# Attention and maxout feed-forward on one core: bias products as units of their own, first loads in quarters, twelve result buffers, and a new queue

## The chip, the cores and the metric

The kernel runs on one core of a Trainium2 chip. Its time is the device time of one execution in microseconds (us), lower is better. A profile is one execution taken by the hardware profiler; engines are called TensorE (PE, with PEld for its weight loads), VectorE (DVE), ScalarE (ACT), GpSimd (POOL) and SyncE (SP, which here issues nearly all DMAs).

## What is computed

A windowed attention with global keys (4 batches, 8 heads, 768 positions, head size 64), then a feed-forward layer with a maximum over three products. Cut to its core:

```python
scores = scale * q @ k.T                       # 4 x 8 heads, 768 x 768, head size 64
keep   = (pos_k < 8) | ((0 <= rel) & (rel < 96))
bias   = -slopes[h] * where(is_global & ~is_local, 96, abs(rel))
a      = softmax(where(keep, scores + bias, -1e9))
x      = (a @ v) as 3072 x 512
h      = maximum(maximum(x @ w1, x @ w2), x @ w3)    # 3072 x 768
out    = h @ w_out                                    # 3072 x 512, float32
```

## The kernel before, in words

Positions are worked on in 24 tiles T of 128 (six for each batch). A tile needs scores against itself and the tile before it; tile 0 of a batch only against itself. The eight global keys and values of a batch are copied over rows of the preceding tile's keys and values that are out of the window anyway. Tiles are gathered into chunks of 4, 2, 2, 4, 4, 4, 4 for the feed-forward part; `c` below is the chunk, `f` one of six blocks of 128 hidden columns, `j` one of the three weight matrices.

The order of all work is written out by hand (by a planner outside this file) in one string, `SCHEDULE`. Each word is a unit: a letter, its arguments, and after `@` the slot of the ring (buffer) that it writes. Each engine gets its instructions in the order of that string and runs them strictly in that order; semaphores between engines follow from the buffers. The units that matter here:

- `l a.G.p`: load a (0 q, 1 k, 2 v) of the pair of tiles G. The first two pairs of q and k come as one group of four tiles, `QUAD` = 12, split by heads into parts p: 0 and 1 are halves (512 KB), 2 and 3 quarters. `c a.G.p.how` casts it to bf16; `v T.e.how` casts values; `how` is the engine: 0 ScalarE, 1 VectorE, 2 GpSimd.
- `x G.a.p` and `y G.a.p.how`: transposes on TensorE and the copy out of PSUM into `qkT`. Later pairs use `X T`, a transposing DMA.
- `G T.how`, `V T.e.how`: the copies of global keys and values. `G T` has to stand behind the scores of tile T, `V T` behind its products with v.
- `S T.g.how`: scores of four heads (g is 0 or 1). Where `how` is 1, two matmuls with the identity first put the bias into PSUM, and the mask product is not needed.
- `e T.g`: exponential on ScalarE. `m T.g`: product with the mask `wmask`. `A T`: product with v. `n T`: normalization. `t`/`u` or `Z`: transpose of x.
- `K h`, `B h.how`: rows of `wmask` and of `bias`. `D n.w`: n dummy matmuls of width w.
- `w g.j`, `W g.j.how`: load and cast of weights (g = 0: 256 columns, 512 KB, blocks f 0 and 1; g = 1: 512 columns, 1 MB, cast in two units W1 and W2 for blocks 2, 3 and 4, 5). `q`, `Q`: the same for w_out.
- `F c.f.j` (four matmuls, "gate product") and `f c.f.j.how`: the products of the three matrices and the maximum. `O c.tt` (six matmuls), `o` and `s`: the product with w_out of one tile, the copy out of PSUM, the store. `E`: the products, copies and stores of the last chunk in one unit, the last tile in pieces of 256, 128 and 128 columns; the last piece's store goes out from ScalarE's queue.

Result tiles lie in the staging rings of the weights, `wst0` and `wst1`, of three slots each.

Of the kernel before, what the change touches and what calls it, by code (L numbers as in the profile page):

```python
# [29 lines left out]
    v2.1.1 v2.0.1 A0@0 n0@0 v3.0.2 l2.2.2@2 w1.1@1 A1@4 V1.1.2 e2.0@5 v3.1.2 n1@1 S3.0.1@6 c0.2.2.0@2 V1.0.1  # L30
    S3.1.1@0 w1.2@2 t1@2 c1.2.2.1 u1.1@0 e3.0@6 A2@4 n2@2 x2.0.2@3 V2.1.2 V2.0.2 x2.1.2@2 G3.2 y2.1.2.1@2
    e3.1@7 l1.3.2@6 A3@0 t2@4 l0.3.2@0 y2.0.2.0 W0.1.2 n3@3 t0@3 u2.0 S4.0.0@6 u0.1 e4.0@1 S4.1.0@4 t3@2
    u3.1 W0.0.1 G4.2 S5.0.0@0 W0.2.2 e5.0@3 S5.1.0@6 m5.0.1 V3.1.0 e5.1@0 m5.1.1 m4.0.1 W2.0.1 v5.0.2 e4.1@2
    W1.0.1 F0.0.1@2 F0.1.1@3 F0.0.0@0 f0.0.0.0@0 F0.1.0@1 F0.0.2@4 F0.1.2@0 f0.1.0.0@1 F0.4.0@1 v5.1.2
    V3.0.1 F0.3.0@5 m4.1.1 f0.0.1.1 f0.1.1.1 f0.1.2.1@0 v4.0.0 v4.1.0 F0.2.0@2 f0.3.0.0@2 A4@6 F0.5.0@0
    V4.0.0 l2.3.2@0 W2.1.1 W1.1.2 q1@0 W1.2.0 F0.4.1@3 l1.4.2@1 f0.0.2.1 n4@1 F0.5.1@4 c1.3.2.2@1 V4.1.1
    f0.2.0.0@3 A5@6 f0.4.0.1@4 F0.3.1@1 l0.4.2@2 t4@5 n5@2 F0.2.1@6 t5@2 F0.3.2@7 f0.5.0.0@1 F0.2.2@0 u4.1@1
    f0.2.1.1 f0.3.1.1 f0.5.1.1 u5.0 c0.3.2.0 F1.0.1@1 F1.4.0@2 x3.0.2@6 F1.2.0@4 W2.2.0 f0.2.2.1 f0.4.1.1
    f1.4.0.0@0 q2@1 f0.3.2.1 v6.1.2 v7.0.2 q0@2 y3.0.2.0@3 F1.0.0@0 f1.0.0.0@3 f1.0.1.1 F1.4.1@5 v6.0.2
    l2.4.2@1 x3.1.2@7 Q1.2 l1.5.2@3 F0.5.2@0 c1.4.2.2@0 F1.0.2@1 v7.1.2 f1.4.1.1 y3.1.2.0 G6.0 c0.4.2.2  # L40
    f1.2.0.0@2 f0.5.2.1 f1.0.2.1@1 F1.2.1@5 f1.2.1.1 Q0.2 S6.0.0@2 e6.0@4 l0.5.2@4 S7.0.0@6 S7.1.0@0
    S6.1.0@4 F0.4.2@2 f0.4.2.1 e7.1@5 F1.5.0@3 F1.1.0@0 m7.1.1 e7.0@6 m7.0.1 F1.3.0@1 F1.5.1@2 x4.1.2@6
    f1.5.0.0@1 F1.2.2@3 m6.0.1 f1.2.2.1 v8.1.2 l1.6.2@5 e6.1@7 m6.1.1 x4.0.2@7 f1.5.1.1 f1.1.0.0@3 F1.1.1@0
    f1.1.1.1 f1.3.0.0@4 y4.1.2.0@0 A7@4 V7.0.2 v9.0.2 G7.0 v9.1.2 F1.3.1@1 n7@0 y4.0.2.0 Q2.0 c1.5.2.0@2
    F1.4.2@0 f1.4.2.1 f1.3.1.1 F1.5.2@2 S8.1.0@4 S8.0.0@6 f1.5.2.1 G8.0 A6@0 O0.2@2 n6@3 O0.3@3 e8.1@1 Z7@2
    o0.3.1@0 e8.0@2 o0.2.0@0 t6@0 c0.5.2.2 v8.0.2 u6.1 m8.1.1 V7.1.1 m8.0.1 O0.1@1 o0.1.1@1 S9.1.0@2 e9.1@0
    m9.1.1 S9.0.0@4 G9.1 e9.0@3 F2.0.0@0 F2.5.0@6 F1.1.2@7 F1.3.2@1 F2.3.0@2 f1.1.2.1 m9.0.1 l2.5.2@2 A8@4
    v11.1.0 V8.0.0 V8.1.2 F2.2.0@3 f2.3.0.0@2 f2.2.0.0@0 f2.5.0.1@1 f1.3.2.1 n8@1 l0.6.2@6 F2.3.1@7 f2.3.1.1
    F2.2.1@1 f2.2.1.1 F2.4.0@6 c0.6.2.0@1 f2.0.0.0@3 A9@2 n9@2 v10.1.1 c1.6.2.2 X10@1 S10.0.0@4 e10.0@5
    V9.1.1 m10.0.1 S10.1.0@0 e10.1@6 V9.0.0 G10.1 O1.1@7 F2.5.1@2 f2.5.1.1 t8@3 F2.4.1@0 O0.0@1 m10.1.1 X11  # L50
    S11.1.0@4 l1.7.2@0 f2.4.0.0@4 o1.1.0@2 e11.1@4 v11.0.0 u8.1@0 S11.0.0@2 v10.0.1 f2.4.1.1 A10@6 V10.0.2
# [37 lines left out]
RINGS = {'r': 7, 'rv': 3, 'qb': 3, 'qkT': 4, 'sp': 2, 'h': 8, 'P': 8, 'xb': 4, 'xT': 3, 'wst0': 3, 'wst1': 3, 'ht': 2, 'h01': 5, 'rz': 4}  # L89

LAST_BANKS = (7, 6, 4, 5, 2, 0, 3, 1)

LAST_STAGES = ((2, 1, 0), (2, 0, 1))


@with_exitstack
def kernel(
# [13 lines left out]
    nc = tc.nc  # L111
# [24 lines left out]
    for name in RINGS:  # L136
        if name not in ("h", "sp"):
            pools[name] = ctx.enter_context(tc.tile_pool(name=f"p_{name}", bufs=1))
# [42 lines left out]
    def cast(how, dst, src):  # L181

        n = src.shape[1]
        for lo, hi in (((0, n // 2), (n // 2, n)) if how == 2 else ((0, n),)):
            copies[how](dst[:, lo:hi], src[:, lo:hi])  # L185
# [400 lines left out]
```

## Time and profile before

| what | value |
|---|---|
| time, median of 3 runs (lowest, highest) | 176.48 us (176.45, 177.07) |
| the profiled execution's own time | 176.6 us |
| its span, first to last instruction | 174.7 us |
| busy, share of the span: PE, DVE, ACT, POOL | 96%, 73%, 59%, 28% |
| granted TensorE clock, mean | 1.000 |
| instructions | 3862 |

Times in the profile count from the span's start. A row of a group reads: line, engine, operation, tiles, count, then busy us in all and mean ns of one, then the engine's idle time just before them with what ended it.

### The profile page before, as it was taken

The page shows a single profiled execution, that of the slowest core. Times are in us where ns is not written, and L with a number is a line of the kernel's source. Part 1 is how long each engine was busy: PE and PEld are TensorE (multiplying, and loading weights), DVE is VectorE, ACT ScalarE, POOL GpSimd, SP SyncE. Part 2 cuts the span into 40 slices and gives each one's busy share as a digit, 9 for nine tenths or more (in the row PEclk, how much of TensorE's full clock was granted, in tenths as well). Part 3 has the DMA queues.
Part 4 walks back from the last instruction along what each step waited for, and adds up shares of the span by engine and source line. Part 5 has one row for each costly group of instructions (what it writes and reads, how often), then busy time and mean ns, then how long its engine had stood idle before and what let it go on. Part 6 is the DMA issues. An engine that isn't in the chain of part 4 may idle for free.

```text
span 174.7 us, 3862 instructions
## 1 busy us (share of the span) xinstructions
PE 166.9 (96%) x1489; PEld 93.5 (54%) x1510; DVE 127.7 (73%) x259; ACT 102.4 (59%) x153; POOL 48.9 (28%) x94
## 2 busy tenths in 40 slices
PE   7799999999999999999999999999999999999992
PEld 2346745576956867644456445554444554444442
DVE  7798969784868988589697287839859993059930
ACT  5979895487995876746257994721375651310022
POOL 4056536349370300196614003200203210000000
PEclk9999999999999999999999999999999999999999
DMA  5999999999999898998989498999992134047106
GB/s 148 352 292 312 363 351 379 294 319 345 270 230 267 193 145 194 290 319 198 232 146 196 119 253 200 290 159 260 272 184 68 32 90 64 0 180 240 60 10 234
DMA packets 66658, 37.35 MB, mean 214 GB/s; under 512 B 24144, under 2 KB 61904, under 8 KB 66640
## 3 DMA queue, kind: packets, MB, share of 16 engines
q1 hardware_dynamic: 66496, 37.04, 84.5%
q8 instruction: 12, 0.20, 0.5%
q10 hardware_dynamic: 144, 0.07, 0.1%
q14 instruction: 6, 0.05, 0.1%
HBM read 25.17 MB, written 6.29 MB: 180 GB/s over the span
## 4 chain that ended last, share of the span: by engine, by line
PE 83%; DVE 5%; DMA 4%; ACT 3%; issue 2%; SPq 1%; ACTq 0%
PE psum L405 50%; PE psum L429 18%; PE psum L321 5%; DMA rawqq<-in_q_dram 4%; PE psum L363 4%; PE psum L366 3%; PE psum L258 2%; DVE qkT L266 1%; ACT P L328 1%; PE psum L390 1%; DVE h L421 1%; DVE P L337 1%; PE psum L313 1%; SPq L213 1%; ACT qb L185 1%
## 5 line engine op out<-in xcount | busy, mean ns | idle before, releaser
L405 PE MATMUL psum<-xT,w 128*128 128x512 bf16 (+1 forms) x491 | 99.3, 348 | 1.1
L405 PEld LDWEIGHTS <-w 128*128 128x128 bf16 x504 | 47.5, 98 | 43.1 <-issue 2.7
L328 ACT ACTIVATE P<-psum 128x1024 bf16<-128x1024 f32 (+1 forms) x48 | 43.3, 953 | 13.5 <-PE psum L321 13.2
L421 DVE TENSOR_TENSOR h<-h,psum 128x512 bf16<-128x512 bf16 (+1 forms) x42 | 24.6, 604 | 16.1 <-PE psum L405 12.6
L429 PE MATMUL psum<-wo,ht 128*128 128x512 bf16 (+2 forms) x148 | 32.9, 362 | 0.6 <-issue 0.3
L337 DVE TENSOR_TENSOR P<-P,wmask 128x1024 bf16<-128x1024 bf16 x35 | 23.8, 695 | 6.2 <-ACT P L328 6.1
L424 DVE TENSOR_TENSOR ht<-h,psum 128x512 bf16<-128x512 bf16 (+1 forms) x42 | 26.1, 643 | 3.0 <-PE psum L405 2.4
L419 ACT CAST h<-psum 128x512 bf16<-128x512 f32 (+1 forms) x32 | 15.6, 517 | 20.1 <-PE psum L405 17.9
L429 PEld LDWEIGHTS <-ht 128*128 128x128 bf16 x156 | 14.0, 98 | 14.1
L238 POOL CAST va<-rawv 64x512 bf16<-64x512 f32 x26 | 16.5, 636 | 13.6 <-DMA rawv<-in_v_dram 12.8
L375 DVE TENSOR_TENSOR xb<-psum,rz 128x512 bf16<-128x512 f32 x24 | 16.6, 691 | 0.8
L299 POOL COPY va<-vaf 4x260 int32<-4x260 int32 x15 | 5.9, 395 | 37.5 <-PE psum L366 37.2
L321 PE MATMUL psum<-qkT 64*128 64x128 bf16 x352 | 14.9, 217 | 1.2 <-DVE qkT L266 0.9
L321 PEld LDWEIGHTS <-qkT 64*128 64x128 bf16 x352 | 10.3, 94 | 9.6 <-issue 6.8
L363 PEld LDWEIGHTS <-P 128*128 128x128 bf16 x192 | 12.3, 97 | 2.4
L363 PE MATMUL psum<-va,P 128*128 128x65 bf16 x160 | 12.5, 193 | 0.1
L444 ACT COPY ost<-psum 128x512 f32<-128x512 f32 x11 | 6.4, 589 | 8.9 <-PE psum L429 8.2
L366 PEld LDWEIGHTS <-P 128*128 128x128 bf16 x160 | 10.4, 97 | 1.5 <-issue 0.3
L434 ACT COPY ost<-psum 128x512 f32<-128x512 f32 (+2 forms) x5 | 2.3, 480 | 15.1 <-PE psum L429 15.0
L366 PE MATMUL psum<-va,P 128*128 128x65 bf16 x128 | 9.9, 193 | 0.0
L301 ACT COPY va<-vaf 4x520 bf16<-4x520 bf16 x10 | 6.2, 620 | 3.8 <-PE psum L366 3.7
L374 DVE RECIPROCAL rz<-psum 128x8 f32<-128x8 f32 x24 | 4.8, 202 | 4.7 <-PE psum L366 3.7
(69 smaller groups left out, 134.4 us busy)
## 6 DMA issues: line engine op xcount, KB each, us to landing
rawv<-in_v_dram SPq DMA_DIRECT2D x12, 512.0 KB, 6.3
rawq<-in_q_dram SPq DMA_DIRECT2D x10, 512.0 KB, 7.3
rawk<-in_k_dram SPq DMA_DIRECT2D x10, 512.0 KB, 7.0
out_dram<-ost SPq DMA_DIRECT2D x19, 256.0 KB, 2.6
wst<-in_moe_w_dram SPq DMA_DIRECT2D x3, 1024.0 KB, 10.9
wst<-in_moe_w_dram SPq DMA_DIRECT2D x3, 512.0 KB, 8.1
wost<-in_moe_w_out_dram SPq DMA_DIRECT2D x3, 512.0 KB, 7.3
out_dram<-ost SPq DMA_DIRECT2D x9, 128.0 KB, 1.8
```

The lines of the kernel that those rows point to most:

```text
L238: copies[how](heads(va(T))[64 * e:64 * e + 64, :, 0:D], src)
L321: nc.tensor.matmul(sp[:, hh, j2, ds], qT(T - ds, 1)[hsl, jp], qT(T, 0)[hsl, jp], start=not how, stop=True, skip_group_check=True)
L328: nc.scalar.activation(P[:, :, 0:n], sps[T, g].rearrange("p a b d n -> p (a b) d n")[:, :, 0:n], AF.Exp, bias=0.0, scale=scale)
L337: mul(P, P, wmask[:, g, :, 0:2])
L363: nc.tensor.matmul(o, P[:, i, 0], heads(va(T))[:, h], start=True, stop=(t == 0), skip_group_check=True)
L366: nc.tensor.matmul(o, P[:, i, 1], heads(va(T - 1))[:, h], start=False, stop=True, skip_group_check=True)
L375: nc.vector.tensor_tensor(out=x.rearrange("p (g h) d -> p g h d", g=2), in0=o4[:, :, :, 0:64], in1=rz[:, :, :, None].to_broadcast([128, 2, ...
L405: nc.tensor.matmul(ps, w123[f // 2][:, j, dm, (f % 2) * 128:(f % 2) * 128 + 128], xT[c][:, dm], start=(dm == 0), stop=(dm == 3))
L419: copies[how](h01, ps)
L421: nc.vector.tensor_max(h01s[c, f], h01s[c, f], ps)
L424: nc.vector.tensor_max(dst, h01s[c, f].rearrange("p (t e i) -> p t e i", e=2, i=64), ps.rearrange("p (t e i) -> p t e i", e=2, i=64))
L429: nc.tensor.matmul(po, ht[c][:, f, tt * 128:(tt + 1) * 128], wo[:, f, cols], start=(f == 0), stop=(f == NF - 1))
```

## The change

- A new unit `b T.g` holds the two bias matmuls of a score unit; it takes the PSUM slot, and `S T.g.1` then adds the scores onto it. The seven biased units are 0.0, 0.1, 1.0, 2.0, 2.1, 3.0, 3.1, as before.
- The second loads of q and k of `QUAD` (part 0) are replaced by two quarters each (parts 2 and 3), with their casts and transposes; `cast` can split a quarter for GpSimd.
- Results are copied to a ring `os` of twelve buffers of 512 columns, which lies over the memory of `wst1`; `wst0` and `wst1` become parts of one tile `staging`.
- `SCHEDULE`, `LAST_BANKS` and `LAST_STAGES` are new. Dummy matmuls: before `D10.512 D3.256 D3.256`, then `D10.512 D1.256 D3.256 D3.256 D3.256 D2.256`. In the middle casts and copies change engines (fewer on GpSimd), and at the end one whole result tile of chunk 5 (`O5.0 o5.0.0 s5.0.2`) stands behind `E`.

```diff
 SCHEDULE = """
-    l0.12.1@0 l1.12.1@1 R K4 K3 K6 B4.1 B0.1 K5 K0 K2 B1.0 K7 B6.0 B2.1 l1.12.0@2 B3.1 c0.12.1.1@0 B7.1
-    l0.12.0@3 l2.0.2@0 l2.1.2@1 l0.2.2@4 c1.12.1.1@1 l1.2.2@5 w0.1@0 B5.1 D10.512@0 w0.0@1 x12.0.1@0
-    y0.0.1.0@0 w0.2@2 D3.256@1 x12.1.1@1 y0.1.1.1 S0.1.1@2 c1.12.0.1 c0.12.0.1 S1.1.0@4 K1 x12.1.0@6
-    y0.1.0.1 G0.2 y1.0.1.0@1 e1.1@0 m1.1.1 v0.0.2 v1.0.2 e0.1@1 v0.1.2 D3.256@0 x12.0.0@0 y0.0.0.0 S1.0.1@2
-    w1.0@0 G1.0 e1.0@2 y1.1.0.1 S0.0.1@4 e0.0@3 y1.1.1.1 y1.0.0.1 S2.1.1@6 e2.1@4 v1.1.2 S2.0.1@2 G2.2
...
+    l0.12.1@0 l1.12.1@1 R K7 D10.512@0 l1.12.2@2 l0.12.3@3 l1.12.3@4 l0.12.2@5 K3 K0 K5 K1 K2 K6 K4 B6.1
+    B1.0 B7.2 B5.1 c0.12.1.1@0 D1.256@0 x12.0.1@0 B2.1 B4.1 c1.12.1.1@1 B0.0 c1.12.2.2 l2.0.2@0 b0.1@2
+    x12.1.1@1 y0.0.1.1@0 l2.1.2@1 b2.1@4 y0.1.1.0 D3.256@6 S1.1.0@6 c0.12.3.1 y1.0.1.0@1 S0.1.1 c1.12.3.2
+    v0.1.2 y1.1.1.1 v1.1.2 v0.0.2 v1.0.2 e1.1@0 l1.2.2@6 c0.12.2.1 B3.1 x12.1.2@0 x12.0.3@1 x12.1.3 x12.0.2
+    y0.1.0.0 l0.2.2@0 b1.0@6 y0.0.0.1 S1.0.1 G0.1 G1.1 e0.1@1 y1.0.0.1 b0.0@2 S2.1.1 m1.1.1 y1.1.0.0 S0.0.1
+    b2.0@0 S2.0.1 v3.1.2 e1.0@2 e0.0@3 e2.1@4 v2.1.1 G2.1 w0.0@0 v2.0.1 b3.0@2 w0.1@1 e2.0@5 D3.256@6 A1@4
+    V1.0.1 A0@6 v3.0.2 c1.2.2.2@2 V1.1.1 w1.0@0 n1@0 S3.0.1 b3.1@0 S3.1.1 e3.0@6 e3.1@7 t1@4 G3.0 n0@1
+    l2.2.2@2 A2@2 V2.0.2 w0.2@2 V2.1.2 t0@5 u0.0@0 c0.2.2.1 w1.1@1 x2.1.2@6 n2@2 x2.0.2@7 y2.1.2.0@2
+    y2.0.2.1 A3@0 w1.2@2 u1.0 n3@3 D3.256@2 S4.1.0@2 e4.1@0 l1.3.2@1 S4.0.0@4 G4.1 t2@6 u2.0 W0.0.1 t3@7
...
-    f6.0.1.1 f6.0.2.1 f6.3.2.1 s4.0.2 s4.3.2 s5.2.2 F6.5.0@0 f6.5.0.1@0 F6.5.1@3 f6.5.1.1 F6.5.2@1 f6.5.2.1 E@0
+    f6.1.1.1 f6.1.2.1 F6.2.2@0 F6.5.0@2 f6.2.2.1 f6.5.0.1@1 F6.5.1@1 f6.5.1.1 f6.5.2.1 o5.2.1@9 s5.2 s4.3.2
+    E@3 O5.0@1 o5.0.0@6 s5.0.2
 """
-RINGS = {... 'wst0': 3, 'wst1': 3, ...}
+RINGS = {... 'wst0': 3, 'wst1': 3, ..., 'os': 12}
-LAST_BANKS = (7, 6, 4, 5, 2, 0, 3, 1)
-LAST_STAGES = ((2, 1, 0), (2, 0, 1))
+LAST_BANKS = (5, 4, 3, 0, 2, 7, 6, 1)
+LAST_STAGES = (11, 0, 4, 1, 10, 3, 2, 7, 8, 9, 5, 6)
...
+    staging = persist.tile([128, 2048 * RINGS["wst1"] + 1024 * RINGS["wst0"]], FP32, name="staging")
+    staged = {"wst1": (0, 2048), "os": (0, 512), "wst0": (2048 * RINGS["wst1"], 1024)}
...
-    def u_S(slot, T, g, how):
-        t = T % NT
+    def u_b(slot, T, g):
+
+        n = 2 if T % NT else 1
         sp = ring("sp", slot, [128, 2, 2, 2, 128], FP32, "sp")
         sps[T, g] = sp
-        n = 2 if t else 1
+        for hh in range(2):
+            nc.tensor.matmul(sp[:, hh, :, 0:n], identb, bias[:, g, hh, :, 0:2] if n == 2 else bias[:, g, hh, :, 2:3],
+                             start=True, stop=False, skip_group_check=True)
+
+    def u_S(slot, T, g, how):
+        n = 2 if T % NT else 1
         biased[T, g] = how
-        if how:
-            for hh in range(2):
-                nc.tensor.matmul(sp[:, hh, :, 0:n], identb,
-                                 bias[:, g, hh, :, 0:2] if t else bias[:, g, hh, :, 2:3],
-                                 start=True, stop=False, skip_group_check=True)
+        if not how:
+            sps[T, g] = ring("sp", slot, [128, 2, 2, 2, 128], FP32, "sp")
+        sp = sps[T, g]
...
     def u_o(slot, c, tt, how):
-
-        osts[c, tt] = ring(("wst0", "wst1")[chunks[c][tt] % 2], slot, [128, DM], FP32, "ost")
+        osts[c, tt] = ring("os", slot, [128, DM], FP32, "ost")
```

More of the change, by code (lines that the diff above doesn't have):

```diff
@@ L30 @@
[L30 to L39, printed above, removed]
@@ new lines @@
+    F1.2.0@4 m7.0.1 f1.2.0.0@0 x4.1.2@2 y4.1.2.0@0 x4.0.2@3 y4.0.2.0 A6@0 n6@2 F1.1.1@4 Q2.0 f1.1.1.1
+    F0.2.1@6 l0.6.2@1 F1.1.2@2 A7@0 t6@3 u6.0@2 f0.2.1.1 F0.2.2@4 n7@3 S8.0.0@0 Q0.0 S8.1.0@6 f0.2.2.1
+    f1.3.2.1 t7@3 u7.1 e8.0@0 F1.4.1@4 f1.4.1.1 e8.1@3 F1.4.2@5 f1.1.2.1 F1.2.1@3 c1.5.2.0@2 G8.1 f1.4.2.1
+    l2.5.2@2 f1.2.1.1 F2.1.0@4 F2.2.0@2 F2.3.0@3 c0.5.2.1 f2.2.0.0@2 F1.2.2@5 f2.3.0.0@1 S9.0.0@0 Q1.1
+    S9.1.0@2 v9.0.0 e9.0@1 e9.1@2 O0.1@6 F2.3.1@7 O0.0@0 o0.1.0@0 X10@1 m8.0.1 F2.4.0@1 c0.6.2.0@1 m8.1.1
@@ L86 @@
+    f6.2.0.1@2 F6.2.1@1 F6.0.0@0 F6.3.2@4 f6.3.0.0@1 f6.0.0.0@4 f6.0.1.1 f6.3.1.1 f6.2.1.1 F6.4.2@0 F6.0.2@3
+    F6.4.1@1 f6.4.1.1 f6.3.2.1@0 o5.1.0@2 f6.4.2.1 s5.1 s3.0 F6.1.1@2 s5.3 F6.1.2@1 f6.0.2.1 F6.5.2@7
+    f6.1.1.1 f6.1.2.1 F6.2.2@0 F6.5.0@2 f6.2.2.1 f6.5.0.1@1 F6.5.1@1 f6.5.1.1 f6.5.2.1 o5.2.1@9 s5.2 s4.3.2
+    E@3 O5.0@1 o5.0.0@6 s5.0.2
 """
 SIZES = [4, 2, 2, 4, 4, 4, 4]
-RINGS = {'r': 7, 'rv': 3, 'qb': 3, 'qkT': 4, 'sp': 2, 'h': 8, 'P': 8, 'xb': 4, 'xT': 3, 'wst0': 3, 'wst1': 3, 'ht': 2, 'h01': 5, 'rz': 4}
@@ L91 @@
-LAST_BANKS = (7, 6, 4, 5, 2, 0, 3, 1)
-LAST_STAGES = ((2, 1, 0), (2, 0, 1))
+RINGS = {'r': 7, 'rv': 3, 'qb': 3, 'qkT': 4, 'sp': 2, 'h': 8, 'P': 8, 'xb': 4, 'xT': 3, 'wst0': 3, 'wst1': 3, 'ht': 2, 'h01': 5, 'rz': 4, 'os': 12}
+LAST_BANKS = (5, 4, 3, 0, 2, 7, 6, 1)
+LAST_STAGES = (11, 0, 4, 1, 10, 3, 2, 7, 8, 9, 5, 6)
 @with_exitstack
@@ L136 @@
     for name in RINGS:
-        if name not in ("h", "sp"):
+        if name not in ("h", "sp", "wst0", "wst1", "os"):
             pools[name] = ctx.enter_context(tc.tile_pool(name=f"p_{name}", bufs=1))
@@ L157, in ring @@
         assert 0 <= slot < RINGS[name]
+        if name in staged:
+            first, width = staged[name]
+            first += slot * width
+            flat = staging[:, first:first + math.prod(shape[1:])]
+            return flat if len(shape) == 2 else flat.rearrange("p (i f) -> p i f", i=shape[1])
         return pools[name].tile(shape, dtype, name=label, tag=f"{name}{slot}")
@@ L181, in cast @@
     def cast(how, dst, src):
-        n = src.shape[1]
-        for lo, hi in (((0, n // 2), (n // 2, n)) if how == 2 else ((0, n),)):
-            copies[how](dst[:, lo:hi], src[:, lo:hi])
+        if how != 2:
+            copies[how](dst, src)
+            return
+        first = src.shape[1] > 1
+        n = src.shape[1 if first else 2] // 2
+        for half in (slice(0, n), slice(n, 2 * n)):
+            s = (slice(None), half) if first else (slice(None), slice(None), half)
+            copies[how](dst[s], src[s])
     def words(ap):
@@ L461, in stage @@
             o[0] += 1
-            name = ("wst0", "wst1")[o[0] % 2]
-            return ring(name, LAST_STAGES[o[0] % 2][(o[0] - 1) // 2 % RINGS[name]], [128, DM], FP32, "ost")[:, 0:w]
+            return ring("os", LAST_STAGES[(o[0] - 1) % len(LAST_STAGES)], [128, DM], FP32, "ost")[:, 0:w]
         po = [bank(DM) for _ in range(min(2, n - 1))]
@@ L539, in u_R @@
         nc.vector.tensor_copy(rbase[:, 0], rel[:, 1])
-    units = {"l": u_l, "c": u_c, "v": u_v, "x": u_x, "y": u_y, "X": u_X, "G": u_G, "V": u_V, "S": u_S,
+    units = {"l": u_l, "c": u_c, "v": u_v, "x": u_x, "y": u_y, "X": u_X, "G": u_G, "V": u_V, "b": u_b, "S": u_S,
              "e": u_e, "m": u_m, "B": u_B, "K": u_K, "A": u_A, "n": u_n, "t": u_t, "u": u_u, "Z": u_Z,
```

91 lines of the change are left out of this document (46 added, 45 removed).

## The prediction

> **What bounds the kernel now.** I read the page's first two parts first, then busy time by stretch of the span, then the chain that ended last and the timelines of its two ends. The numbers in a row of stretches are its length, then each engine's busy time.
>
> ```profile
> PE 166.9 (96%) x1489; PEld 93.5 (54%) x1510; DVE 127.7 (73%) x259; ACT 102.4 (59%) x153; POOL 48.9 (28%) x94
> PEclk9999999999999999999999999999999999999999
> 0.00:21.50 21.50, 18.68 (x238) 10.76 (x238) 17.75 (x51) 17.83 (x29) 8.89 (x24) 1.00 1.01 292
> 21.50:166.20 144.70, 142.88 (x1221) 79.74 (x1238) 108.22 (x206) 82.24 (x120) 40.02 (x70) 1.00 0.86 207
> 166.20:174.70 8.50, 5.30 (x36) 2.98 (x35) 1.71 (x3) 2.30 (x5) 0.00 (x0) 1.00 0.36 125
> 35.00:50.00 15.00, 14.82 (x179) 11.54 (x179) 11.71 (x24) 13.05 (x21) 9.35 (x17) 1.00 1.07 304
> ```
>
> TensorE is the bound, at full granted clock. From 21.5 to 166.2 us it is busy 142.88 of 144.70 us: only 1.8 us are idle there, so a better order can win at most that much in the middle. What else can be won lies in the first 21.5 us and in the last three. The fourth row is the one stretch where VectorE, ScalarE and GpSimd together are heavily loaded; it returns below.
>
> ```profile
> 2.33 7.04 DMA rawqq<-in_q_dram
> 9.39 0.69 DVE qbq L185
> 10.09 0.60 DVE qkT L266
> 10.69 0.60 DVE P L337
> 11.29 1.80 DVE qkT L266 x3
> 13.14 0.40 PE psum L321 x8
> 19.50 0.59 ACT xT L393
> 21.97 7.50 PE psum L405 x34
> ```
>
> This is the chain's start. The second q load lands at 9.4; its cast, one copy out of PSUM, a mask product and three more copies follow one another on VectorE; then TensorE works almost without a break until the gate products (L405) run back to back, 7.50/34 = 0.22 us each.
>
> **The change, part by part.**
>
> *Bias products ahead.* The same seven score units use them (14 matmuls before and after, all for tiles 0 to 3), so no TensorE work goes. They now run while TensorE waits for the copies into qkT. ScalarE gets all eight mask exponentials and two bias rows ahead of its first such copy.
>
> ```profile
> 3.50 2.59 ACT L350 ACTIVATE wmask<-rbase 128x384 bf16<-128x384 f32 x6 [1.27 <-DVE rbase L539]
> 7.11 0.62 PE L252 MATMUL psum<-identb,qbq 128*128 128x128 bf16 x8 [0.42 <-DVE qbq L185]
> 7.77 0.69 DVE L266 COPY qkT<-psum 128x512 bf16<-128x512 bf16 x1 [0.45 <-PE psum L252]
> 10.14 0.62 PE L252 MATMUL psum<-identb,qbq 128*128 128x128 bf16 x8
> 9.58 0.49 PE L506 MATMUL psum<-zeros 128*128 128x256 bf16 x3
> 25.25 1.29 DVE L185 CAST w<-wst 128x1024 bf16<-128x1024 f32 x2
> ```
>
> Ten such instructions at 2.59/6 = 0.43 from 3.50 end at 7.8, just as the transposes of the first k half (7.11 + 0.62) are done: they cost nothing as long as that half lands no earlier. One bias row (B7) moves to GpSimd, where no row shows that operation; even at 1.2 us, about three times ScalarE's step, it ends by 4.7, ahead of the transposes.
>
> *Quarters.* The second pair of loads is 2 x 512 KB in four pieces, the same bytes; its last piece lands when the last half did, 9.4. What follows it is half as wide: of the cast's 0.69 about 0.3 goes, and of the transposes' 0.62 about 0.2 (four fewer at 0.06). Of the chain above, the mask product (0.60) now stands behind, and of the four copies one runs before the landing and one on ScalarE (1.2). Against that, a copy of global keys (G1) on VectorE now waits for the scores of tile 1, and the last copy stands behind it: some 0.8. Net, tile 2's scores start about 1.3 us sooner than 13.1 (between 0.3 and 1.7). SyncE issues two more DMAs; nothing hurries there, as transfers queue behind one another.
>
> *What takes the lead then.* Weights. The fifth gate product in the new order reads block w1.0. That load moves from fourth to third of the weight loads, so one 512 KB transfer sooner: at the 292 GB/s of the first stretch, 1.8 us. Its cast starts at 25.25 now, so 23.5 then, and the product at 23.5 + 0.7 + 0.1 = 24.3 at the earliest. Before, TensorE had done four gate products of four matmuls at 25.0 (the row of 34 starts at 21.97 with two matmuls ahead of it, so 21.55, and 16 x 0.216 on). Of the gain at the start at most 0.7 therefore survives. Six more dummy matmuls come in (L506, steps of (0.49 - 0.27)/2 = 0.11 us each with the 0.27 us of the row below); four stand where TensorE waits anyway, the last two (0.2) directly ahead of that fifth product. I take **-0.4**, ends -0.7 and +1.0 (the load comes no earlier: 25.25 + 0.8 = 26.0).
>
> *The end.* The new list ends with E and then a whole tile of chunk 5: six products, a copy of 128x512 on ScalarE and two stores of 128 KB from SyncE. Before, E was last, and it closes with a 128-column piece whose store goes out from ScalarE.
>
> ```profile
> L506 PE MATMUL psum<-zeros 128*128 128x256 bf16 x6 | 1.0, 273 | 0.0
> 169.63 1.93 PE psum L429 x20
> 171.63 0.27 ACT ost L434
> 171.93 0.37 ACTq L435 DMA_DIRECT2D out_dram<-ost  x1
> L434 ACT COPY ost<-psum x5: 265/586/592, 168.8 to 171.6; 128x512 f32<-128x512 f32 x3, 128x256 f32<-128x256 f32 x1, 128x128 f32<-128x128 f32 x1
> 169.41 2.79 SPq L435 DMA_DIRECT2D out_dram<-ost  x5
> out_dram<-ost SPq DMA_DIRECT2D x9, 128.0 KB, 1.8
> out_dram<-ost ACTq DMA_DIRECT2D x1, 64.0 KB, 1.8
> ```
>
> TensorE ends at 171.56 and does the same work in either order. After it, before: copy 0.27, store issued at 171.93, landed 1.8 later, close. Then: copy 0.59 (+0.3), first store issued, the second behind it (+0.4, an issue on this queue taking 0.33 to 0.45), landed 1.8 later. Sum **+0.8**; ends +0.3 (the second issue hidden) and +1.2 (E's own stores still in the way). Nothing covers it: it is the last thing in the program.
>
> *Twelve result buffers.* The list of waits has no copy to a result buffer that waited for a store:
>
> ```profile
> ACT ost L444 <- PE psum L429: 8.2, 3, 3.3
> DVE ost L444 <- PE psum L429: 2.2, 2, 1.7
> ```
>
> They waited for TensorE. So the buffers by themselves are worth nothing; they free the planner to put stores late. The new ring lies over the large weight staging; in the list that one's last cast stands far ahead of the first result.
>
> *The queue planned anew.* This is the large unknown. By unit names, GpSimd's 34 casts of v become 12, its 16 half-casts of q and k 10, its 10 halves of weights none, its 15 copies of global v 6.
>
> ```profile
> L337 DVE TENSOR_TENSOR P<-P,wmask 128x1024 bf16<-128x1024 bf16 x35 | 23.8, 695 | 6.2 <-ACT P L328 6.1
> L238 POOL CAST va<-rawv x26: 606/612/1077, 12.0 to 139.3; 64x512 bf16<-64x512 f32 x26
> L238 ACT CAST va<-rawv x8: 612/618/622, 26.6 to 131.1; 64x512 bf16<-64x512 f32 x8
> L185 ACT CAST qb<-rawk x3: 1045/1045/1046, 49.3 to 81.9; 128x1024 bf16<-128x1024 f32 x3
> L185 DVE CAST qb<-rawk x2: 674/678/682, 16.7 to 118.4; 128x1024 bf16<-128x1024 f32 x2
> L337 DVE TENSOR_TENSOR P<-P,wmask x35: 666/682/1092, 10.6 to 142.4; 128x1024 bf16<-128x1024 bf16 x35
> L339 DVE TENSOR_TENSOR P<-P,wmask x6: 417/574/828, 45.7 to 110.4; 128x512 bf16<-128x512 bf16 x6
> ```
>
> Unit by unit at such medians, ScalarE's list gains 18 us and VectorE's 6. Over the span both stay under TensorE (102.4 + 18 and 127.7 + 6 against 166.9), so the price is only paid where both are full at once. The 1.8 us of idle bounds the gain; for the loss I take 2.2 us (worked out under the second rival). Near even, a little on the losing side because two engines now carry what three did: **+0.4**, ends -1.8 and +2.2.
>
> **The sum**, on the profiled execution (176.6 us: a span of 174.7 and 1.9 around it; the median of three is 176.48): 176.6 - 0.4 + 0.8 + 0.4 = **177.4 us**, about 0.5% over. A measurement of this kernel tells some 0.5% (0.88 us) from no change.
>
> **Rivals.**
>
> *Faster: GpSimd out of VectorE's way.* Three mask products out of six at half width took up to 0.828 instead of 0.417, one of the full ones 1.092 instead of 0.682, and GpSimd's casts now and then 1.077 instead of 0.612. If those collisions are what TensorE's idle 1.8 us in the middle come from, they go where GpSimd goes: 176.6 - 0.4 + 0.8 - 1.8 = 175.2. It decides if the middle wins more than 1.3 us. For it: the long durations. Against it: the full mask products have a median of 0.682 and a mean of 0.695, so that hardly more than one of 35 is long (35 x 0.013 = 0.46), although GpSimd was busy 28% of the span, and the bound is TensorE. [...] Chance 0.17.
>
> *Slower by more: VectorE and ScalarE become the bound in one stretch.* Between 35 and 50 us they and GpSimd are busy 11.71 + 13.05 + 9.35 = 34.1 us. In the new list GpSimd has no work there. At some 0.8 of GpSimd's price (a cast of q or k is 1.05 or 0.68 against two halves at 0.61) 7.5 us move over: (11.71 + 13.05 + 7.5)/2 = 16.1 us on each in 15 us, 1.1 over even if perfectly split; two queues in strict order may double it to 2.2: 176.6 - 0.4 + 0.8 + 2.2 = 179.2. Against it: the new list keeps three wide gate products (F0.5.2, F0.2.1, F0.2.2) back as cover. Chance 0.21.
>
> *No change:* the start keeps its 0.7, the second store's issue hides (+0.3) and the middle comes out even: 176.6 - 0.7 + 0.3 = 176.2; with a middle of +0.6, 176.8. I put it at 176.5. Chance 0.22. The forecast's own case (177.0 to 178.0) has 0.40.
>
> **How the numbers follow.** The range of 175.3 to 179.5 leaves out some two thirds of the first rival and what goes beyond the second; the forecast's own case is 177.0 to 178.0. Faster by over 0.5% (under 175.6): most of the first rival, 0.15. Within 0.5% (175.6 to 177.36): the rest of it, the no-change case and a quarter of the forecast's, 0.34. Slower: 0.51.
>
> **What would show it.** Right: the last TensorE matmul of the new profile is followed by a 128x512 copy and two stores, with the span ending 3.7 to 4.2 us after it (3.1 now); the first gate product starts between 20.7 and 21.3; the fifth one between 24.3 and 25.2; TensorE idle in the middle is 1.5 to 3 us. Wrong: waits of TensorE for VectorE or ScalarE between 35 and 50 us of over 2 us (second rival); or a middle with under 0.5 us of idle and mask products all near 0.68 and 0.42 (first rival); or a fifth gate product near 26, if the weights come no sooner.

## The result, and the profile after

The changed kernel takes **180.82 us** (median of 6 runs, 180.47 to 181.56) against 176.46 us for the kernel before: ratio 1.0247, 95% interval 1.0221 to 1.0272. Forecast were 177.4 us, range 175.3 to 179.5. Measured again (the control among the experiments) the ratio is 1.0238 (1.0220 to 1.0256). The profiled execution takes 181.56 us with a span of 179.6, so 4.9 us more span than before; the control's profiled execution has a span of 178.7, 4.0 us more. Slow executions at a clearly lower mean clock are left out of every ratio, but the profiles of the second and fourth experiments are of such executions (0.852 and 0.963), so that times read from these two are rough.

First the page of the changed kernel, then its busy time by stretch (length; busy PE, PEld, DVE, ACT, POOL; granted clock; DMA share; GB/s). The stretches end at its first gate product and at its last products.

```profile
PE 168.4 (94%) x1494; PEld 94.9 (53%) x1516; DVE 132.6 (74%) x280; ACT 117.8 (66%) x180; POOL 19.0 (11%) x40
PEclk9996999999999999999999999999999999999999
0.00:23.90 23.90, 19.81 (x242) 12.17 (x242) 18.09 (x52) 18.14 (x31) 10.79 (x24) 0.93 1.01 305
23.90:170.10 146.20, 143.57 (x1221) 80.00 (x1241) 113.62 (x227) 96.73 (x145) 8.18 (x16) 1.00 0.80 193
35.00:50.00 15.00, 14.68 (x144) 10.43 (x146) 13.90 (x30) 13.26 (x21) 0.00 (x0) 1.00 1.11 323
```

ScalarE is up by 15.4 us and VectorE by 4.9, about what the list of units gave (18 and 6). In the middle TensorE is idle for 146.20 - 143.57 = 2.6 us where it was 1.8. The large loss stands in the first row, which became 2.4 us longer, and in it the clock is no longer full. The chain of waits there, and the gate products (L426) behind it:

```profile
3.34 5.98 DMA rawqq<-in_q_dram
9.35 0.44 DVE qbq L196
10.27 0.70 DVE qkT L283
11.01 0.30 PE psum L342 x4
11.34 0.57 DVE qkT L308
11.90 0.59 DVE qkT L283
12.54 0.30 PE psum L342 x4
12.87 0.25 ACT qkT L283
13.35 1.53 ACT P L349 x2
14.93 0.73 PE psum L328 x2
12.87 0.58 ACT L283 COPY qkT<-psum 128x512 bf16<-128x512 bf16 x1 [2.05 <-PE psum L342]
23.99 3.61 PE L426 MATMUL psum<-xT,w 128*128 128x512 bf16 x15
27.66 1.67 PE L426 MATMUL psum<-xT,w 128*128 128x512 bf16 x7
```

The last quarter is cast at 9.35 in 0.44 us, and tile 2's scores start at 12.54, 0.6 us sooner than before (13.14). Up to here the prediction's walk holds. Then ScalarE, which had been idle for 2.05 us, makes a copy into qkT (`y1.1.0.0`) that stands in the list behind these scores, and only behind that copy four exponentials (L349) that A1 and the score banks of TensorE wait for. The bias product at 14.93 is waiting for one of them. The fifth gate product (the second row of L426) starts at 27.66, not at 24.3 to 25.2.

The clock, by stretch: two rows of the changed kernel; two of the control (the same program) with its first gate products; one of the kernel before:

```profile
10.00:15.00 5.00, 2.90 (x39) 1.52 (x38) 3.86 (x9) 2.95 (x6) 3.50 (x5) 1.00 1.20 290
16.00:18.00 2.00, 2.00 (x34) 1.73 (x32) 0.73 (x3) 0.71 (x1) 1.04 (x2) 0.50 1.10 384
```
```profile
10.00:15.00 5.00, 2.90 (x39) 1.52 (x37) 3.86 (x9) 2.95 (x6) 3.51 (x5) 1.00 1.20 290
15.00:20.00 5.00, 4.43 (x79) 3.07 (x78) 3.65 (x10) 3.96 (x6) 2.52 (x4) 1.00 1.10 370
23.51 2.75 PE L423 MATMUL psum<-xT,w 128*128 128x512 bf16 x11
```
```profile
10.00:15.00 5.00, 4.58 (x67) 2.49 (x67) 4.43 (x9) 4.31 (x8) 3.59 (x7) 1.00 1.20 290
```

Between 10 and 15 us TensorE is busy for 2.90 us instead of 4.58, in both executions of the changed kernel alike. In the profiled one the granted clock then falls to 0.50, in the control's it stays at 1.00, and there the first gate product comes at 23.51 instead of 23.99. So the waiting costs about 2 us in both of these executions, and in one of them the clock takes about half a us more. The clock fell here with no wait over 0.81 us; the waits made 2.1 us together in 5 us. Why it fell in one execution of the program and not in the other is not shown.

The end: the chain, and the stores' queue, of the changed kernel.

```profile
170.65 4.53 PE psum L450 x32
175.20 0.58 ACT staging L464
175.81 0.81 SPq L470 DMA_DIRECT2D out_dram<-staging  x2
```

TensorE ends at 175.18 and the span at 179.6: 4.4 us, against 3.1 before. In the control it is 174.74 to 178.7, 4.0 us.

How the 4.0 us of the control split over the span is seen when the same amount of TensorE work is looked up in each trace (all matmuls in their order, each counted with the median spacing of its kind, narrow dummies left out). The columns are times in the kernel before; a cell says how many us later the work done by then is reached:

| kernel | at 24.8 us | at 52.5 | at 80.3 | at 118.8 | at 166.4 |
|---|---|---|---|---|---|
| changed, profiled first | 2.45 | 3.57 | 3.23 | 3.52 | 3.61 |
| changed, control | 1.97 | 3.11 | 2.77 | 3.09 | 3.17 |
| y1.1.0.0 ahead (first experiment) | 1.24 | 2.36 | 2.02 | 2.31 | 2.40 |
| start in order (fifth) | 0.74 | 1.85 | 1.51 | 1.83 | 1.91 |
| v of tiles 4 on to GpSimd (seventh) | 1.95 | 2.41 | 3.10 | 3.21 | 3.30 |
| start, tail, v of tiles 4 to 7 (ninth) | 0.77 | 1.23 | 0.81 | 1.10 | 1.12 |
| and the rest of the start (twelfth) | 0.22 | 0.68 | 0.27 | 0.57 | 0.59 |

For the control: start +2.0, middle +1.2, and 178.7 - 174.7 - 3.17 = +0.8 at the end. (A single cell can be some tenths off, because the two orders do different work at that point.)

### The profile page after: what moved, and what is told of

It is laid out like the page before. It is cut to its first block, busy times and chain, and to the rows that moved or that the text cites. A ratio compares the mean times of both kernels' runs of the same rounds, so it can differ in the third digit from the quotient of the medians.

```text
span 179.6 us, 3853 instructions
## 1 busy us (share of the span) xinstructions
PE 168.4 (94%) x1494; PEld 94.9 (53%) x1516; DVE 132.6 (74%) x280; ACT 117.8 (66%) x180; POOL 19.0 (11%) x40
## 4 chain that ended last, share of the span: by engine, by line
PE 70%; ACT 7%; DMA 7%; DVE 7%; SPq 4%; issue 3%; DVEq 0%; ACTq 0%
PE psum L426 42%; PE psum L450 14%; PE psum L342 5%; DMA rawk<-in_k_dram 3%; DMA rawqq<-in_q_dram 3%; ACT P L349 3%; PE psum L384 3%; SPq L237 2%; PE psum L387 2%; PE psum L275 2%; SPq L230 1%; DVE xb L396 1%; PE psum L411 1%; DVE ht L445 1%; DVE h L442 1%
## 5 line engine op out<-in xcount | busy, mean ns | idle before, releaser
L426 PE MATMUL psum<-xT,w 128*128 128x512 bf16 (+1 forms) x489 | 98.5, 348 | 1.3 <-DVE ht L445 0.2
L426 PEld LDWEIGHTS <-w 128*128 128x128 bf16 x504 | 47.8, 98 | 43.9 <-issue 3.0
L349 ACT ACTIVATE P<-psum 128x1024 bf16<-128x1024 f32 (+1 forms) x48 | 43.9, 956 | 6.5 <-PE psum L342 6.0
L440 ACT CAST h<-psum 128x512 bf16<-128x512 f32 (+1 forms) x29 | 14.8, 531 | 14.2 <-PE psum L426 13.0
L464 ACT COPY staging<-psum 128x512 f32<-128x512 f32 x15 | 8.8, 588 | 8.0 <-PE psum L450 4.2
L384 PEld LDWEIGHTS <-P 128*128 128x128 bf16 x192 | 13.0, 100 | 1.8
L440 DVE CAST h<-psum 128x512 bf16<-128x512 f32 (+1 forms) x13 | 7.8, 602 | 7.6 <-PE psum L426 7.4
L255 ACT CAST va<-rawv 64x512 bf16<-64x512 f32 x20 | 12.3, 620 | 0.8 <-DMA rawv<-in_v_dram 0.4
L196 ACT CAST qb<-rawk 128x1024 bf16<-128x1024 f32 x6 | 6.3, 1048 | 9.1 <-DMA rawk<-in_k_dram 9.1
L316 POOL COPY va<-vaf 4x260 int32<-4x260 int32 x6 | 2.4, 395 | 93.3 <-PE psum L387 89.4
L387 PEld LDWEIGHTS <-P 128*128 128x128 bf16 x160 | 10.8, 99 | 1.6 <-issue 0.2
L455 ACT COPY staging<-psum 128x512 f32<-128x512 f32 (+2 forms) x5 | 2.3, 480 | 11.0 <-issue 10.2
```

The source lines that it names most:

```text
L255: copies[how](heads(va(T))[64 * e:64 * e + 64, :, 0:D], src)
L349: nc.scalar.activation(P[:, :, 0:n], sps[T, g].rearrange("p a b d n -> p (a b) d n")[:, :, 0:n], AF.Exp, bias=0.0, scale=scale)
L384: nc.tensor.matmul(o, P[:, i, 0], heads(va(T))[:, h], start=True, stop=(t == 0), skip_group_check=True)
L387: nc.tensor.matmul(o, P[:, i, 1], heads(va(T - 1))[:, h], start=False, stop=True, skip_group_check=True)
L426: nc.tensor.matmul(ps, w123[f // 2][:, j, dm, (f % 2) * 128:(f % 2) * 128 + 128], xT[c][:, dm], start=(dm == 0), stop=(dm == 3))
L440: copies[how](h01, ps)
```

## The experiments

All ratios are to the kernel before on the same chip. The experiments' lists take three lines less, so that a line of the changed kernel has a number lower by 3 there (L283 is L280). Where two 95% intervals overlap, the two kernels are not told apart by their times. First the control and single parts.

**Control.** The changed kernel again.

> The changed kernel as it is, again, as the measure for the runs beside it: ratio to the kernel before 1.0247 as measured first, so about 181 us. No theory says otherwise.

Ratio 1.0238 (1.0220 to 1.0256).

**1. One copy ahead of the scores.**

```diff
-y1.0.0.1 b0.0@2 S2.1.1 m1.1.1 y1.1.0.0 S0.0.1
+y1.0.0.1 y1.1.0.0 b0.0@2 S2.1.1 m1.1.1 S0.0.1
```

> The changed kernel with one unit moved: ScalarE's copy of the first k half of the second pair into qkT (y1.1.0.0) stands ahead of the second tile's scores S2.1.1 instead of behind them. Theory (the queue order costs the start): ScalarE's wait of 2.05 us goes, the exponentials of tiles 1, 0 and 2 and with them A1 come 1.0 to 1.5 us sooner, the granted clock no longer falls to 0.50, the first gate product starts at about 21.9 instead of 23.95; time 178.3 to 178.9 against 180.8. Rival (the falling clock alone costs it, the wait is covered): the wait goes, the clock falls all the same, under 0.7 us gained. Rival (the start is bound by loads): no gain.

Ratio 1.0189 (1.0167 to 1.0210), 0.9 to 1.0 us less than the changed kernel. ScalarE's timeline, and a stretch:

```profile
10.80 0.59 ACT L280 COPY qkT<-psum 128x512 bf16<-128x512 bf16 x1
11.55 1.02 ACT L346 ACTIVATE P<-psum 128x1024 bf16<-128x1024 f32 x1 [0.15 <-PE psum L339]
15.00:20.00 5.00, 4.19 (x86) 3.27 (x84) 4.27 (x10) 3.71 (x6) 3.21 (x6) 1.00 1.10 370
22.77 1.46 PE L423 MATMUL psum<-xT,w 128*128 128x512 bf16 x6
```

The copy runs at 10.80 instead of 12.87, the exponential behind it at 11.55 instead of 13.35, and the clock stays full. The first gate product is at 22.77, 0.74 us sooner than the control's at the same full clock. That the copy's place cost time is shown; its size was about half of what I expected. The rival of the falling clock does not fit: over 0.7 us are gained, and the control's profiled execution was late at full clock.

**2. The tail of chunk 5 ahead of E.**

```diff
-E@3 O5.0@1 o5.0.0@6 s5.0.2
+O5.0@3 o5.0.0@6 s5.0.2 E@3
```

> The changed kernel with the tile of chunk 5 (product O5.0, its copy and its two stores) ahead of E instead of behind it; E's last piece ends the program again. Theory from the two traces: the time from TensorE's end to the end of the span falls from 4.42 to 3.1 us, time 179.5 (-1.3). By the term of the prediction (+0.8): 180.0. Rival (the stores of 128 KB still in flight hold E's last store up): 180.4 or more.

Ratio 1.0264 (1.0241 to 1.0287): nothing won, the theory's 1.3 us not borne out; the time is the rival's. The order in SyncE's queue:

```profile
187.19 3.70 SPq L467 DMA_DIRECT2D out_dram<-staging  x5
190.99 2.39 SPq L453 DMA_DIRECT2D out_dram<-staging  x5
```

Five late stores of chunks 4 and 5 now stand right ahead of E's five in the same queue. That suggested experiment 6. That the late stores held up E's last one is not shown by this.

**3. The clock alone.**

```diff
-b0.0@2 S2.1.1
+D7.256@2 b0.0@2 S2.1.1
-b3.0@2
+D5.256@6 b3.0@2
```

> The changed kernel with twelve dummy matmuls of 256 columns more in the places where TensorE waits in 11 to 15 us (seven ahead of b0.0, five ahead of b3.0); no wait is taken away. Theory (the clock is a cost of its own): the granted clock stays at 1.00 between 15 and 19 us, A1 takes 0.55 instead of 1.06 us, the first gate product comes 1.0 to 1.5 us sooner, time 179.3 to 179.8. Rival (the wait alone costs, slow matmuls are covered by the engines that wait beside them): 180.6 to 181.2 even at full clock. Rival (the dummies stand in the way): over 181.2.

Ratio 1.0226 (1.0205 to 1.0248), not told apart from the changed kernel. TensorE is kept busier and the clock is full:

```profile
10.00:15.00 5.00, 4.15 (x51) 2.61 (x50) 3.86 (x9) 2.95 (x6) 3.50 (x5) 1.00 1.20 290
15.00:20.00 5.00, 4.44 (x80) 3.13 (x78) 3.65 (x10) 3.96 (x6) 2.49 (x5) 1.00 1.10 368
23.55 2.75 PE L423 MATMUL psum<-xT,w 128*128 128x512 bf16 x12
```

Its first gate product is where the control's is, at full clock. The rival holds: the wait costs the 2 us, the clock about half a us in the one profiled execution in which it fell.

**4. All engines as before, the new order.**

```diff
-(70 units v, V, c, W on the engines of the changed kernel)
+(the same units, in the same places, on the engines of the kernel before)
```

> The changed kernel, order untouched, with the engine that the kernel before used for every cast of v, of later q and k and of weights and for every copy of global v (24 casts of v go back to GpSimd, 8 of q and k to GpSimd, 3 halves of weights). Theory of the prediction (two engines carry what three did, this costs the middle): the middle gets 0.5 to 1.0 us shorter, 179.8 to 180.3. Rival (the middle is lost to the order, not to the engines): 180.5 to 181.1. Rival (GpSimd out of VectorE's way was worth something): over 181.3.

Ratio 1.0725 (1.0688 to 1.0763), far beyond every expectation; only the last rival (over 181.3) has the direction. From GpSimd's list of waits:

```profile
POOL va L313 <- PE psum L384: 34.4, 8, 11.2
POOL qkT L305 <- PE psum L339: 22.0, 1, 22.0
```

A copy on GpSimd waits up to 22 us for TensorE, and the casts behind it stand still with it. That this is the cause is argued, not shown: in the changed kernel a copy of global values on GpSimd waits 78.7 us, and with 19.0 us of work on that engine it need hold up little. An order is planned for its engines; this run does not tell load from order. Experiment 7 narrows it down.

**5. The start's queues in order.** Beside the edit of experiment 1:

```diff
-G0.1 G1.1 e0.1@1 y1.0.0.1
+G0.1 e0.1@1 y1.0.0.1 G1.1
-V1.0.1 A0@6 v3.0.2 c1.2.2.2@2 V1.1.1
+V1.0.0 A0@6 v3.0.2 c1.2.2.2@2 V1.1.0
```

> The changed kernel with the start's queues put in order: y1.1.0.0 ahead of S2.1.1 (as in the first experiment, which won 0.6% and left the first gate product at 22.63), besides y1.0.0.1 ahead of G1.1 on VectorE, and the two copies V1.0 and V1.1 on ScalarE instead of VectorE, where they stood ahead of n1. Theory (the rest of the start's loss is queue order too): S2.1.1 starts near 12.0 instead of 12.7, n1 no longer waits, TensorE's 0.81 us ahead of t1 goes, the first gate product comes at 21.5 to 21.9; 178.9 to 179.3 against about 181. Rival (what is left is the weight or the v load, or TensorE's own extra dummies): first gate product stays near 22.6, time as in the first experiment, 179.9.

Ratio 1.0172 (1.0145 to 1.0199). Tile 2's scores start at 11.65 us (theory 12.0), but the first gate product is at 22.26, between theory (21.5 to 21.9) and rival (22.6). The time is 1.2 us below the control; the theory wanted 1.7 to 2.1, the rival 1.1, so by time the rival is nearer. The times of this and the first experiment are not told apart; by the table the further edits won 0.5 us.

**6. Results stored early.**

```diff
-f6.5.2.1 o5.2.1@9 s5.2 s4.3.2 E@3 O5.0@1 o5.0.0@6 s5.0.2
+f6.5.2.1 E@3
-f6.4.2.1 s5.1 s3.0 F6.1.1@2 s5.3
+f6.4.2.1 s5.1 s3.0 o5.2.1@9 s4.3 O5.0@5 o5.0.0@6 F6.1.1@2 s5.3 s5.2 s5.0
```

> The changed kernel with its late results staged early: O5.0 and its copy stand ahead of F6.1.1, the copy o5.2 directly behind f6.4.2, and the stores of chunks 4 and 5 leave before E, so that only E's own stores are left behind it. Moving O5.0 alone ahead of E had won nothing. Theory (stores still under way at the end hold the last one up): time from TensorE's end to the end of the span 3.1 instead of 4.42 us, 1.2 us less than the changed kernel beside it. Rival (TensorE gets as much idle elsewhere, or the store's cost is not from the stores ahead of it): under 0.5 us.

(Stores that left in two parts leave as one.) Ratio 1.0196 (1.0179 to 1.0213), 0.75 us below the control, between theory (1.2) and rival (under 0.5). Its end:

```profile
174.60 0.27 ACT L452 COPY staging<-psum 128x128 f32<-128x128 f32 x1 [0.30 <-DMA out_dram<-staging]
174.90 0.37 ACTq L453 DMA_DIRECT2D out_dram<-staging  x1
172.43 2.80 SPq L453 DMA_DIRECT2D out_dram<-staging  x5
```

Only E's stores are left, the last copy is narrow again, and the span ends at 178.1, 3.5 us after TensorE (4.0 in the control). The late stores and the wide last tile taken away together give this back; the tile alone gave nothing (second experiment), and the stores alone were not tried.

**7. Only the casts of v on GpSimd.**

```diff
-(34 casts v4.0 to v23.1 with how 0 or 1)
+(the same with how 2)
```

> The changed kernel with only its 34 casts of v for tiles from 4 on moved from ScalarE and VectorE to GpSimd (nothing else changes engine, unlike the fourth experiment, which moved copies of global v and casts of q and k too and lost some 5%). Theory of the prediction (two engines carry what three did): TensorE's idle in 35 to 165 us falls by 0.5 to 1.0 us and the time with it. Rival (GpSimd collides with VectorE's products of two SBUF operands): more mask products over 0.8 us, time up by 0.5 to 2 us. Rival (load is not what costs the middle): within 0.4 us of the changed kernel beside it.

Ratio 1.0210 (1.0195 to 1.0225), 0.5 us below the control, not told apart from it; the two profiled spans are equal within 0.1 us. In the table it gains 0.7 us up to 52.5 and loses it behind. VectorE's mask products (L355) and GpSimd's casts in that stretch, and then the same two rows of the control:

```profile
54.83 6.09 POOL L252 CAST va<-rawv 64x512 bf16<-64x512 f32 x7 [4.96 <-DMA rawv<-in_v_dram]
54.99 2.12 DVE L355 TENSOR_TENSOR P<-P,wmask 128x1024 bf16<-128x1024 bf16 x2
59.68 1.78 DVE L355 TENSOR_TENSOR P<-P,wmask 128x1024 bf16<-128x1024 bf16 x2
```
```profile
55.69 1.29 DVE L355 TENSOR_TENSOR P<-P,wmask 128x1024 bf16<-128x1024 bf16 x2
59.57 1.29 DVE L355 TENSOR_TENSOR P<-P,wmask 128x1024 bf16<-128x1024 bf16 x2
```

The theory and the first rival are both in it. Up to 52.5 us the casts are better on GpSimd. Where four mask products run beside them, two products take 2.12 and 1.78 us instead of 1.29, and the seven casts 0.87 us each instead of 0.61. VectorE's other work is longer there too (a cast of k 0.99 us instead of 0.69, a copy of global v 0.70 instead of 0.28). Up to 62.4 us TensorE then waits 0.48 us for a maximum on VectorE, a wait that the control does not have, and what it had won is gone.

**8. The queue before, in the new code.**

```diff
-(before) S0.1.1@2 ... o0.3.1@0
+(after)  b0.1@2 S0.1.1 ... o0.3.1@0, o0.2.0@1, ... one slot after the other
```

> The queue of the kernel before, unit by unit, in the changed kernel's code: its bias products written as units of their own directly ahead of their scores, its results in the twelve staging buffers, one after another. Only the buffers and the code differ from the kernel before. Prediction's price (buffers and separate bias units are worth nothing by themselves): 1.000, within 0.3% of the kernel before. Rival (the shared staging ring adds waits): 0.5% or more over.

Ratio 0.9991 (0.9974 to 1.0009). Buffers and separate bias units are worth nothing by themselves, in the old order.

**9. Start, tail and four tiles' v together.** The edits of 5 and 6, and the casts of v for tiles 4 to 7 on GpSimd.

> The changed kernel with the start's order (fifth experiment: -1.34 us), the early tail (sixth: -0.94) and the casts of v of tiles 4 to 7 alone on GpSimd (the seventh, with all tiles from 4 on, stood 0.44 to 0.7 us ahead of its control up to 54 us and lost 1.35 between 54 and 61 us, where seven casts on GpSimd met four mask products). Theory (three separate losses, that add): 181.0 - 1.34 - 0.94 - 0.7 = 178.0, ratio about 1.007. Rival (they cover one another, or GpSimd's casts collide here too): 178.6 or more.

Ratio 1.0053 (1.0034 to 1.0071), 177.83 us; expected were 178.0. The three losses are separate and add, as far as the spread of the single runs tells. What TensorE still waits for at the start:

```profile
PE psum L381 <- POOL va L252: 0.6, 1, 0.6
PE psum L381 <- ACT P L346: 0.6, 1, 0.6
```

(These two rows are from the fifth experiment's list of waits, which has the same start.) The first is A1, behind GpSimd's fourth cast of v; the second A2, behind the two copies V1 that I had put on ScalarE.

**10. Without eight dummies.**

```diff
-D3.256@6 A1@4 ... D3.256@2 S4.1.0@2 ... D2.256@2 F0.2.0@2
+A1@4 ... S4.1.0@2 ... F0.2.0@2
```

> The kernel of the run beside it (start, tail and v in order) without the eight dummy matmuls ahead of A1, of S4.1.0 and of F0.2.0. Theory (dummies cost their 0.11 us each where TensorE has other work ready; the two ahead of F0.2.0 for certain, by the position of the work, the three ahead of S4.1.0 partly): 0.3 to 0.5 us less than the run beside it. Rival (they keep the clock up, without them the granted clock falls in 15 to 20 us): 0.3 us more or worse.

Ratio 1.0048 (1.0029 to 1.0066): no difference from the ninth in time, so neither the theory nor the rival is borne out. Its trace is 0.23 us later than the ninth's from 8 us on, before any of the edits, and even with it from 29 us on: the dummies ahead of the fifth gate product cost about the 0.2 us that the prediction gave them. The clock did not fall without them (mean 1.000 in the profiled execution).

**11. One mask product later, in the kernel before.**

```diff
-e1.1@0 m1.1.1 v0.0.2 ... y1.0.0.1 S2.1.1@6
+e1.1@0 v0.0.2 ... y1.0.0.1 m1.1.1 S2.1.1@6
```

> The kernel before with one unit moved: the mask product of tile 1, which stands in its chain at the start ahead of three copies into qkT on VectorE, stands behind them, directly ahead of S2.1.1 in the list. Theory (the prediction's walk of the start: VectorE's queue sets when tile 2's scores start): S2.1.1 about 0.6 us sooner, the first gate product at 21.0 instead of 21.5, time 0.3 to 0.6 us under the kernel before. Rival (weights or the exponentials are next): no change, or the wait moves to A1, which needs the product: no change.

Ratio 0.9993 (0.9976 to 1.0009): no change, as the rival says. The gate products of this run, and of the kernel before:

```profile
21.34 8.09 PE L403 MATMUL psum<-xT,w 128*128 128x512 bf16 x35
24.96 1.61 PEld L403 LDWEIGHTS <-w 128*128 128x128 bf16 x8 [0.27 <-issue]
22.96 1.94 ACT L326 ACTIVATE P<-psum 128x1024 bf16<-128x1024 f32 x2
```
```profile
21.52 7.94 PE L405 MATMUL psum<-xT,w 128*128 128x512 bf16 x35
```

The first one is 0.18 us sooner, but the same 35 matmuls last 0.15 us longer. A gap of 0.27 us stands in the fifth product's weight loads. That product (F0.0.2) writes the PSUM slot 4, which the scores S4.1 had before; they are read by the second exponential of the third row, which ends at 24.90, and in the trace it is this exponential that releases the product's first matmul, at 24.91. ScalarE's two exponentials start at 22.96 us, in the kernel before at 22.98: they did not come sooner, and so took the gain back. It is the rival's second case, with the exponentials next and not the weights.

**12 and 13. The two waits left.**

```diff
-v0.0.2 v1.0.2 e1.1@0 ... S2.1.1 m1.1.1
+v0.0.2 e1.1@0 ... S2.1.1 m1.1.1 v1.0.1
-A1@4 V1.0.0 A0@6 v3.0.2 c1.2.2.2@2 V1.1.0
+A1@4 A0@6 v3.0.2 V1.0.2 V1.1.2 c1.2.2.2@2
```

> The kernel of the ninth experiment (start, tail and v in order, 0.5% over the kernel before) with the two waits that its trace still shows at the start taken away: the cast v1.0, the last of four on GpSimd, for which A1 waited 0.65 us, goes to VectorE behind m1.1.1, where VectorE idles; the copies V1.0 and V1.1 go from ScalarE, where they stood 1.26 us ahead of the exponential that A2's bank waited for (0.63 us), to GpSimd. Theory (the whole loss at the start is queue order): first gate product about 21.3 instead of 22.3, then the cast of w1.0 (landing 23.3) sets the fifth at 24.7; 0.7 to 1.1 us less than the ninth, ratio 0.999 to 1.002 of the kernel before. Rival (the next load or engine queue is as late: GpSimd's c1.2 or VectorE's n's): under 0.4 us.

> The kernel beside it without the eight dummy matmuls ahead of A1, S4.1.0 and F0.2.0, which made no difference while the start was late. Theory (they cost where TensorE has no wait left to fill): another 0.2 to 0.4 us, ratio 0.997 to 1.000. Rival (the weights' cast sets the fifth gate product with or without them, or the clock falls): no change or slower.

Twelfth: ratio 1.0031 (1.0008 to 1.0054), the first gate product at 21.76 (22.30 in the ninth). By the table 0.55 us come back, by the ratios 0.4 and by the medians 0.7: theory (0.7) and rival (under 0.4) are not told apart. One more queue shows in its trace: up to 18.1 us TensorE waits 0.52 us for GpSimd's cast c1.2, as the rival had it. Thirteenth, without the eight dummies: 1.0009 (0.9998 to 1.0020), 177.01 us against 176.87, not told apart from the twelfth; the theory's 0.997 is not reached. Its own trace starts 0.2 us later than the twelfth's (a load), and it still ends even with it. The changed kernel, put in order at these few places, is as fast as the kernel before; no version was measurably faster than the kernel before.

## Why the prediction was right and wrong

**The start, -0.4: wrong, and this is the step that failed.** Up to tile 2's scores the walk along VectorE was right in kind: separate bias products at nothing (eighth experiment), the mask and bias rows on ScalarE done at 7.7 us (7.8 forecast), quarters at 0.44 us a cast, tile 2's scores 0.6 us sooner, in the range of 0.3 to 1.7. (The forecast was 1.3; the terms listed for it add up to 1.5.) The failed step is "of the four copies one runs before the landing and one on ScalarE (1.2)" with what follows from it, "What takes the lead then. Weights." The copy moved to ScalarE was taken off the chain without a look at ScalarE's own queue. There it stands behind the scores S2.1.1 and ahead of four exponentials, so that it came last of all and delayed them (first experiment: 0.9 to 1.0 us of time, 0.7 by position). And behind VectorE's chain I let only the weights lead and looked for no other queue. The runs showed three queues there: ScalarE's, VectorE's (the copy of global keys G1.1, the copies V1) and GpSimd's (the fourth cast of v). Taken together the edits of experiments 1, 5 and 12 move the position at 24.8 us from 1.97 to 0.22. The term was +2.0 us, not -0.4.

That `y1.1.0.0` waited for scores of the other four heads, whose data it does not touch but whose tile it writes into, is what the release in the trace says. Why the program has that dependency was not tried by itself.

**The weights as the next limit: not borne out.** The load of w1.0 did land sooner, at 22.9 us instead of 25.2 (2.3 us, forecast 1.8). But its cast started at 25.7 in the changed kernel, not at 23.5, because VectorE's queue came to it only then, and TensorE came to the fifth product only at 27.66: the start's own queues were later than the weights. In the kernel before, a gain of 0.2 us at the first gate product was lost again at the fifth, to an exponential on ScalarE (eleventh experiment).

**The clock: left out.** It fell to 0.50 in one of two profiled executions, behind the stretch with the waits, and cost about half a us there (first gate product at 23.99 against 23.51).

**The end, +0.8: right in size.** 4.0 us from TensorE's end in the control, 3.7 to 4.2 forecast; 4.4 in the first profile. The terms show too: a copy of 0.59 us and two issues of 0.81 together in the control, and in the first profile the last two stores land 2.2 us after their issue (1.8 forecast). But moving O5.0 alone does not win it back (second experiment): the late stores had to go as well, which the prediction named ("to put stores late") and did not price.

**The middle, +0.4: right in kind, undersized.** +0.8 by idle time, +1.2 by position, with 2.6 us idle (forecast 1.5 to 3). By the table nearly all of it arises between 24.8 and 52.5 us. About half of it is the second rival's mechanism at a quarter of its price: casts of v of tiles 4 to 7 on ScalarE and VectorE, worth 0.6 us at 52.5 us by the table (the ninth experiment against the fifth). No wait of over 2 us appeared in 35 to 50 us. Some 0.2 us are the dummies ahead of the fifth product, which the prediction counted at the start; the remainder is open.

**Faster rival: its mechanism exists, its gain does not.** The mask products became shorter, as the page of the changed kernel shows (695 ns mean before):

```profile
L358 DVE TENSOR_TENSOR P<-P,wmask 128x1024 bf16<-128x1024 bf16 x35 | 23.2, 683 | 1.7 <-ACT P L349 1.5
```

The idle time in the middle did not fall with it (1.8 us before, 2.6 after). Whether some of the old 1.8 us came from collisions is not shown by that, as the new order has waits of its own. In the seventh experiment collisions do cost, where casts and mask products run side by side: 2.12 and 1.78 us for two products instead of 1.29. In the old queue, with 48.9 us of work on GpSimd, hardly more than one of the 35 wide products was long.

**Twelve buffers, bias units: at nothing, as priced** (eighth experiment, in the old order).

## What to carry to other kernels

When a step is moved to another engine to shorten a chain, walk that engine's queue too: what stands ahead of the step there, and what stands behind it and is now held. After a queue has been planned anew, the first places to look are idle rows of a non-bottleneck engine directly ahead of work that the bottleneck waits for; here a handful of moved units gave back 1.75 of the 2 us lost there. An engine assignment and an order belong together: with the old assignment in the new order the kernel was 7% over the kernel before, where the new order with its own assignment was 2.4% over.

## What the runs showed of the hardware

- The granted clock fell to 0.50 and was below full for some 3 us (0.62, 0.50, 0.50 and 0.67 in the four us from 15 to 19) after 5 us in which TensorE was busy for 2.90, with no single wait over 0.81 us; the same program in another execution kept 1.00.
- A mask product of VectorE with two operands in SBUF took 1.06 us instead of 0.65 (2.12/2 against 1.29/2) beside GpSimd's casts, and those 0.87 instead of 0.61. A cast of VectorE with one operand took 0.99 instead of 0.69 us there.
